# Writing the first two segments of the feed-forward loop into the tail of the attention part

## The chip, the cores and the metric

The kernel runs on one core of a Trainium2 chip, in one launch. The metric is the device time of that core in microseconds. Three runs of the kernel before gave a median of 1109.43 us (1109.27 to 1109.46).

## What is computed

Three stages follow each other on a batch of 4 sequences of 576 tokens, 512 channels wide. The first is attention with random features, for 8 heads of 64 channels and 128 features. The second adds the real part of a Fourier transform over tokens and channels, normalises, and runs a two-layer feed-forward net. The third mixes tokens through a matrix of rank 32 and runs a second net.

```
phi(x) = exp(h - max h) / sqrt(128),   h = x omega^T - |x|^2 / 2
x  = phi(q) (phi(k)^T v) / (phi(q) sum phi(k) + 1e-6)
u  = x + real(fft(fft(x, axis=1), axis=2))
un = (u - mean u) / sqrt(var u + 1e-6)
x  = u + relu(un @ w_ch1) @ w_ch2
u  = x + (x^T U V)^T
out = u + relu(u @ w2_ch1) @ w2_ch2
```

The weights are 512 x 2048 and 2048 x 512 and come as 64-bit floats.

## The kernel before

**Precision.** A product in full precision is made of three: each operand is split into a rounded `hi` and a remainder `lo`, and TensorE adds hi hi, hi lo and lo hi. A split is a copy on ACT and a subtraction on VectorE or GpSimd (`split`, line 119; `wsplit` and `sjob` for weights).

**Weights.** A weight tile (128 x 512) is loaded as 64-bit words (`w_load`), converted with integer steps (`conv_a` and `conv_b`, or in the loop `conv_abs`, `w_conv_exp`, `conv_c` and `conv_d`), kept in one of NSTG staging buffers `w`, and split into the buffers of a ring slot. The ring has RING = 5 slots, weight number f, counted through both layers, goes to slot f mod 5. Slots 0 to 2 lie in the pool `mp`, opened when the attention part's pool `pla` closes; slots 3 and 4 lie in `wbp`, opened when all of the attention part is closed. A conversion needs one buffer named `m` and one named `s` of the pool `cv`, which has two of each. CONV lists the stages of the attention part in which the first eight conversions are written.

**Attention part.** The loop over `n` from line 890 on has 36 stages of 128 tokens, 18 for each pair of batches: nine for keys and values, nine for queries. The transform of the pair is written between the stages, as PLAN says: `fold` adds and subtracts rows of x (F and L), `s_stage` is the transform over tokens (S), `d_stage` over channels (D; r0, r2 and r1 are its three parts, called r stages here), whose results GpSimd adds into `uT`. Ten more rounds (n = 36 to 45, written s = 0 to 9) are the tail: they hold the transform of the last two batches, the split of block 0 (`ln_apply`), and the first steps of the loop. In all of this a planner puts the instructions of each engine in an order of its own, by priority (the order of writing) and by what it takes to be ready; a tile has a name and a fixed number of buffers, and waits for one.

**Feed-forward loop.** The tokens are cut into five blocks of 512, 384, 512, 384 and 512 columns (`BLKS`). The hidden width is cut into 16 parts of 128. A unit is one block and one part; four parts make a group, and a segment is one block with the four parts of a group, so units 0 to 3 are block 0, units 4 to 7 block 1, and so on. `l1(i)` is the first product of a unit, 4 groups of 3 matmuls (lines 760 to 762), and evicts it as `hh` (ACT) and `hl` (VectorE). `l2(i)` is the second, 4 groups of 3 (lines 781 to 783) into four accumulators; after the fourth part VectorE multiplies by 1/deviation (`rs`, line 792), in the first layer, and GpSimd adds to `uT` (line 793). `step(i)` writes l1(i+1) and then l2(i). After each group of three matmuls `tick` is called once: it lets the first job of `jobs` go on to its next `yield`, and in every second call the first of `wjobs`.

**Jobs.** `prep_ln(blk)` makes the statistics of a block: column sums (`s1`), split, a matmul with ones for the mean (lines 596 and 597), then the centred copies `c`, x as `hi` and `lo`, the squares summed on GpSimd (line 616), split, a matmul for the variance (lines 632 and 633), square root and reciprocal. A step may begin block b only when x of that block has been written; if not, it calls `tick` until it has. `wjob` converts a weight of the next group, `sjob` splits it.

**Order.** `step(0)` and `step(1)` (TAIL = 2) are written in rounds s = 2 and 3 of the tail. The rest is a section in which TensorE, ACT, VectorE and GpSimd keep the written order, and in front of it slot 3 is split, as its pool opens there.

Of the kernel before, what the change touches and what calls it, by code (L numbers as in the profile page):

```python
# [26 lines left out]
NBX = 512  # L27
# [13 lines left out]
TAIL = 2  # L41
RING = 5
NSTG = 8
CONV = [1, 4, 5, 8, 20, 26, 31, 33]
# [49 lines left out]
def tile_favor_fnet_moe(ctx: ExitStack, tc: tile.TileContext, qT, kT, v1, om, w1a, w2a, uu, vv, w1b, w2b, cs, cd, out):  # L94
# [97 lines left out]
    def wsplit(fi, k, e=nc.gpsimd):  # L192
        if fi >= 2 * NF or (fi, k) in WS:
            return
        slot = fi % RING
        pool = wpools[0 if slot < 3 else 1]
        hi = pool.tile([128, 512], F32R, tag=f"wh{slot}_{k}", name=f"wh{fi}_{k}")
        lo = pool.tile([128, 512], F32R, tag=f"wl{slot}_{k}", name=f"wl{fi}_{k}")
        split(hi, lo, W.pop(2 * fi + k), e)
        WS[(fi, k)] = hi, lo  # L200
# [211 lines left out]
    def d_stage(b, nm):  # L412
# [10 lines left out]
        qs = plf.tile([128, NEO], F32, tag="qs", name=f"qs{b}{nm}")  # L423
        nc.scalar.activation(qs, pq[0], AF.Copy)
        mm = plf.tile([128, NEO], F32, tag="mm", name=f"mm{b}{nm}")
        pm = plf.tile([128, NEO], F32, tag="pmt", name=f"pm{b}{nm}")
# [14 lines left out]
    omh = ac.tile([128, 256], F32R, tag="omh", name="omh")  # L441
    oml = ac.tile([128, 256], F32R, tag="oml", name="oml")
# [134 lines left out]
    def prep_ln(blk):  # L577
# [16 lines left out]
        yield  # L594
        pmn = misc(f"pmn{blk}")[:, 0:nb]
# [3 lines left out]
        mean = lnt("mean", f"mean{blk}")[:, 0:nb]  # L599
        nc.scalar.activation(mean, pmn, AF.Copy)  # L600
        yield
        hi, lo = x_tiles("x", blk)
# [26 lines left out]
        yield  # L629
        yield  # L630
# [4 lines left out]
        RST[blk] = rs = xps[1].tile([128, nb], F32, tag=f"rs{blk}", name=f"rs{blk}")  # L635
# [108 lines left out]
    prep_at = {(0, 0, 0): [lambda b=b: prep_ln(b + 1) for b in range(1, NBLK - 1)], (0, 1, 0): [mix_consts]}  # L744
# [25 lines left out]
    def l2(*idx):  # L770
# [7 lines left out]
        for r in range(4):  # L778
# [5 lines left out]
            if f % GRP == GRP - 1:  # L784
                cuts = [(0, NB)] if i < NU - 1 or r < 3 else [(0, NB // 2), (NB // 2, NB)]
                for q0, q1 in cuts:
                    u = uT[:, r, c0 + q0 : c0 + q1]
                    if l == 0:
                        while blk not in RS:
                            tick()  # L790
                        t = wpools[1].tile([128, NBX], F32, tag="t", name=f"t{i}_{r}", bufs=2)[:, 0:NB]
# [9 lines left out]
    def wjob(j):  # L801
# [6 lines left out]
        conv_d(*b, nc.gpsimd)  # L808
        yield

    def sjob(fi, k):
        slot = fi % RING
        pool = wpools[0 if slot < 3 else 1]
# [9 lines left out]
    CAT0 = [10, 11, 12, 13, 14, 15, 16, 17]  # L823
    wq_at = {}
    for g in range(2 * NG - 1):
        for q in range(2 * GRP):
            wq_at.setdefault(PER * g + (CAT0[q] if g == 0 else 2 * q), []).append(lambda j=2 * GRP * (g + 1) + q: wjob(j))
# [12 lines left out]
    def tick():  # L840
        turn[0] += 1
        advance(jobs)
        if turn[0] % 2:
            advance(wjobs)

    def step(i):
        l, blk, f = units[i]
        if i == TAIL or (f % GRP == 0 and i > TAIL):
            jobs.extend(g() for g in prep_at.get((l, f // GRP, blk), []))
        if i + 1 < NU:  # L850
# [7 lines left out]
        if i < NU - 2:  # L858
# [31 lines left out]
    for n in range(NS + 10):  # L890
# [50 lines left out]
        else:  # L941
# [14 lines left out]
            if s == 1:  # L956
# [6 lines left out]
                jobs.append(prep_ln(1))  # L963
# [5 lines left out]
            elif 1 <= s < 8:  # L969
# [4 lines left out]
    wsplit(3, 0)  # L974
    wsplit(3, 1)
# [94 lines left out]
```

## Time and profile before

| | us |
|---|---|
| median of three runs | 1109.43 |
| the profiled execution | 1108.71 |
| its span, first to last instruction | 1106.9 |
| TensorE busy (matmuls) | 1054.6 |
| VectorE busy | 589.8 |
| GpSimd busy | 422.1 |
| ACT busy | 403.7 |

The span is that of the profiled execution; 1.8 us of its time lie around it. Line numbers (L760) are those of the kernel before. PE is TensorE, DVE VectorE, POOL GpSimd, SP SyncE. The profile models the end of a matmul, so successive ones overlap in its rows; the distance between their starts is what one costs. PEclk is the granted clock of TensorE as a share of 2.4 GHz.

### The profile page before, as it was taken

How to read it: one execution, taken by the hardware profiler on the slowest of the kernel's cores; microseconds unless marked ns; L12 is line 12 of the kernel's file. 1: busy time of each engine (PE TensorE's matmuls, PEld its weight loads, DVE VectorE, ACT ScalarE, POOL GpSimd, SP SyncE). 2: the span in 40 equal slices, each digit the busy share in tenths (PEclk: the TensorE clock that was granted, in tenths of full speed). 3: DMA queues.
4: the chain of work that ended last, by engine and by line, in shares of the span. 5: the costliest groups of instructions: out<-in, count | busy, mean ns of one | idle time of the engine just before them, and what ended most of it. 6: DMA issues, size and time to landing. Idle time of an engine off the chain costs nothing.

```text
span 1106.9 us, 14702 instructions
## 1 busy us (share of the span) xinstructions
PE 1054.6 (95%) x5656; PEld 926.1 (84%) x5656; DVE 589.8 (53%) x1025; ACT 403.7 (36%) x900; POOL 422.1 (38%) x392
## 2 busy tenths in 40 slices
PE   8999999867699899999999999999999999999998
PEld 7989998756678798889989787788888989888996
DVE  5899878765677465345434465573243423332222
ACT  7887686433343232222222334332222222121110
POOL 3467745654426535534373245431411131131000
PEclk9999998969899999999999999999999999999999
DMA  7632410000003022101101110011111101100111
GB/s 245 209 109 78 134 39 1 1 0 1 1 1 115 24 82 69 39 20 57 57 20 58 38 39 20 20 41 55 39 37 57 41 19 58 47 11 1 67 38 66
DMA packets 47573, 56.86 MB, mean 51 GB/s; under 512 B 3024, under 2 KB 39248, under 8 KB 47376
## 3 DMA queue, kind: packets, MB, share of 16 engines
q1 hardware_dynamic: 47216, 53.23, 15.5%
q0 software_dynamic: 288, 2.70, 0.7%
q8 instruction: 44, 0.72, 0.3%
q14 instruction: 25, 0.20, 0.1%
HBM read 51.20 MB, written 4.72 MB: 51 GB/s over the span
## 4 chain that ended last, share of the span: by engine, by line
PE 80%; DVE 10%; POOL 4%; ACT 2%; issue 1%; DMA 1%; SPq 0%; DVEq 0%; ACTq 0%; POOLq 0%
PE ph L762 11%; PE ph L760 11%; PE ph L761 11%; PE acc L781 11%; PE acc L783 10%; PE acc L782 10%; PE kvp L285 3%; PE pn L322 2%; POOL uT L793 2%; PE pj L258 1%; PE pj L259 1%; PE pj L260 1%; DVE rs L638 1%; PE pt L306 1%; DMA raw<-in_w1a_dram 1%
## 5 line engine op out<-in xcount | busy, mean ns | idle before, releaser
L767 DVE SCALAR_TENSOR_TENSOR hl<-ph,hh 128x512 fp32r<-128x512 f32 (+1 forms) x160 | 101.8, 636 | 377.7 <-ACT hh L766 377.6
L766 ACT ACTIVATE hh<-ph 128x512 fp32r<-128x512 f32 (+1 forms) x160 | 88.6, 554 | 510.3 <-PE ph L762 510.1
L781 PE MATMUL acc<-hh,wh 128*128 128x512 f32 (+1 forms) x640 | 238.8, 373 | 2.5 <-DVE t L792 2.2
L783 PE MATMUL acc<-hl,wh 128*128 128x512 f32 (+1 forms) x640 | 237.2, 371 | 0.0
L782 PE MATMUL acc<-hh,wl 128*128 128x512 f32 (+1 forms) x640 | 236.8, 370 | 0.0
L158 POOL TENSOR_TENSOR w<-mc,sc 128x512 uint32<-128x512 uint32 x56 | 74.1, 1323 | 262.5 <-DVE mc L155 262.5
L793 POOL TENSOR_TENSOR uT<-uT,t 128x512 f32<-128x512 f32 (+1 forms) x80 | 101.7, 1302 | 132.7 <-DVE t L792 132.7
L781 PEld LDWEIGHTS acc<-hh,wh 128*128 128x128 f32 x640 | 120.6, 188 | 21.5 <-DVE t L792 3.9
L783 PEld LDWEIGHTS acc<-hl,wh 128*128 128x128 f32 x640 | 120.2, 188 | 17.1 <-DVE hl L767 0.7
L782 PEld LDWEIGHTS acc<-hh,wl 128*128 128x128 f32 x640 | 120.4, 188 | 15.5
L762 PE MATMUL ph<-xh,wl 128*128 128x512 f32 (+1 forms) x320 | 121.1, 378 | 7.9 <-POOL wl L121 4.3
L761 PE MATMUL ph<-xl,wh 128*128 128x512 f32 (+1 forms) x320 | 120.3, 376 | 1.9 <-DVE xl L121 1.9
L760 PE MATMUL ph<-xh,wh 128*128 128x512 f32 (+1 forms) x320 | 121.2, 379 | 0.7 <-ACT wh L120 0.7
L760 PE MATMUL ph<-yh,wh 128*128 128x512 f32 (+1 forms) x320 | 118.7, 371 | 0.0
L762 PE MATMUL ph<-yh,wl 128*128 128x512 f32 (+1 forms) x320 | 118.6, 371 | 0.0
L761 PE MATMUL ph<-yl,wh 128*128 128x512 f32 (+1 forms) x320 | 118.4, 370 | 0.0
L819 POOL TENSOR_TENSOR wl<-w,wh 128x512 fp32r<-128x512 f32 x56 | 72.4, 1309 | 47.3 <-ACT wh L817 40.0
L274 ACT ACTIVATE phi<-pj,mx 128x128 f32<-128x128 f32 x288 | 82.0, 384 | 9.2 <-DVE mx L263 8.4
L762 PEld LDWEIGHTS ph<-xh,wl 128*128 128x128 f32 x320 | 61.2, 191 | 17.5 <-POOL wl L121 4.7
L761 PEld LDWEIGHTS ph<-xl,wh 128*128 128x128 f32 x320 | 61.3, 191 | 10.3 <-DVE xl L121 2.4
L760 PEld LDWEIGHTS ph<-xh,wh 128*128 128x128 f32 x320 | 61.2, 191 | 9.6 <-ACT wh L120 1.1
L762 PEld LDWEIGHTS ph<-yh,wl 128*128 128x128 f32 x320 | 60.1, 188 | 8.2
(647 smaller groups left out, 1781.1 us busy)
## 6 DMA issues: line engine op xcount, KB each, us to landing
raw<-in_w1a_dram SPq DMA_DIRECT2D x16, 512.0 KB, 3.6
raw<-in_w2a_dram SPq DMA_DIRECT2D x16, 512.0 KB, 3.5
raw<-in_w1b_dram SPq DMA_DIRECT2D x16, 512.0 KB, 3.6
raw<-in_w2b_dram SPq DMA_DIRECT2D x16, 512.0 KB, 3.5
vt<-in_v_dram SPq DMA_DIRECT2D x18, 260.0 KB, 4.0
raw<-in_kT_dram SPq DMA_DIRECT2D x18, 256.0 KB, 2.9
raw<-in_qT_dram SPq DMA_DIRECT2D x18, 256.0 KB, 3.1
out_dram<-uT SPq DMA_DIRECT2D x11, 256.0 KB, 2.1
```

Source lines behind the costliest of these rows:

```text
L158: aeng.tensor_tensor(out=dst.bitcast(U32), in0=mu, in1=s, op=ALU.add)
L274: nc.scalar.activation(phi_[n][:, h, :], pss[g][:, hh, :], AF.Exp, bias=mx[:, h : h + 1])
L760: nc.tensor.matmul(ph, wh[:, c], xh[:, r, :], start=(r == 0), stop=False)
L761: nc.tensor.matmul(ph, wh[:, c], xl[:, r, :], start=False, stop=False)
L762: nc.tensor.matmul(ph, wl[:, c], xh[:, r, :], start=False, stop=(r == 3))
L766: nc.scalar.activation(hh, ph, AF.Relu)
L767: nc.vector.scalar_tensor_tensor(out=hl, in0=ph, scalar=0.0, in1=hh.bitcast(F32), op0=ALU.max, op1=ALU.subtract)
L781: nc.tensor.matmul(a[r], wh[:, c], hh, start=(q == 0), stop=False)
L782: nc.tensor.matmul(a[r], wl[:, c], hh, start=False, stop=False)
L783: nc.tensor.matmul(a[r], wh[:, c], hl, start=False, stop=(q == GRP - 1))
L793: nc.gpsimd.tensor_tensor(out=u, in0=u, in1=t, op=ALU.add)
L819: nc.gpsimd.tensor_tensor(out=lo, in0=src, in1=hi.bitcast(F32), op=ALU.subtract)
```

## The change

Units 0 to 7, two segments, are written into the tail: TAIL becomes 7, so steps 0 to 6 stand in rounds s = 2 to 8, and step 7, the first in the section with a kept order, issues l2(7) ahead of l1(8). Ring slot 3 moves to the pool `mp`, and `rs` of block 1 to the pool that opens with it. There are six staging buffers for weights instead of eight, the small tables `omh` and `oml` lie in the pool that closes early, and the r stages' temporaries `qs` and `pm` lie in the conversions' buffers `s` and `m`. The last two of the first eight conversions move from stages 31 and 33 into round s = 1 of the tail, with the split of slot 3 behind them.

`prep_ln` is cut into `prep_lna` (to the mean) and `prep_lnb` (the rest). Both of block 1 run in the tail; of block 2 the first part runs in the tail and the second is queued in step 7; blocks 3 and 4 are queued when block 2 begins. The pauses ahead of the two matmuls with ones grow from two turns to three and five. The products of units below TAIL use a buffer named `ct`.

In the loop `wjobs` go on in every call of `tick` while more than two are queued. The last two of the eight conversions of a group are queued four units later, behind the first splits. The last addition of the conversions for the second group moves from GpSimd to VectorE.

```diff
@@ -38,10 +38,10 @@
-TAIL = 2
+TAIL = 7
-NSTG = 8
-CONV = [1, 4, 5, 8, 20, 26, 31, 33]
+NSTG = 6
+CONV = [1, 4, 5, 8, 20, 26]
@@ -193,7 +193,7 @@
-        pool = wpools[0 if slot < 3 else 1]
+        pool = wpools[0 if slot < 4 else 1]
@@ -420,10 +420,10 @@
-        qs = plf.tile([128, NEO], F32, tag="qs", name=f"qs{b}{nm}")
+        qs = cv.tile([128, 512], F32, tag="s", name=f"qs{b}{nm}")[:, 0:NEO]
-        pm = plf.tile([128, NEO], F32, tag="pmt", name=f"pm{b}{nm}")
+        pm = cv.tile([128, 512], F32, tag="m", name=f"pm{b}{nm}")[:, 0:NEO]
@@ -438,8 +438,8 @@
-    omh = ac.tile([128, 256], F32R, tag="omh", name="omh")
-    oml = ac.tile([128, 256], F32R, tag="oml", name="oml")
+    omh = pla.tile([128, 256], F32R, tag="omh", name="omh", bufs=1)
+    oml = pla.tile([128, 256], F32R, tag="oml", name="oml", bufs=1)
@@ -574,7 +574,7 @@
-    def prep_ln(blk):
+    def prep_lna(blk):
@@ -592,13 +592,20 @@
+        yield
-        mean = lnt("mean", f"mean{blk}")[:, 0:nb]
+        LN[blk] = mean = lnt("mean", f"mean{blk}")[:, 0:nb]
+
+    def prep_lnb(blk):
+        c0, nb = BLKS[blk]
+        u = uT[:, :, c0 : c0 + nb]
+        add = dict(op=ALU.add)
+        mean = LN.pop(blk)
@@ -626,13 +633,13 @@
-        yield
-        yield
+        for _ in range(5):
+            yield
-        RST[blk] = rs = xps[1].tile([128, nb], F32, tag=f"rs{blk}", name=f"rs{blk}")
+        RST[blk] = rs = xps[0 if blk < 2 else 1].tile([128, nb], F32, tag=f"rs{blk}", name=f"rs{blk}")
@@ -741,7 +748,7 @@
-    prep_at = {(0, 0, 0): [lambda b=b: prep_ln(b + 1) for b in range(1, NBLK - 1)], (0, 1, 0): [mix_consts]}
+    prep_at = {(0, 0, 2): [lambda b=b, p=p: p(b) for b in (3, 4) for p in (prep_lna, prep_lnb)], (0, 1, 0): [mix_consts]}
@@ -788,7 +795,7 @@
-                        t = wpools[1].tile([128, NBX], F32, tag="t", name=f"t{i}_{r}", bufs=2)[:, 0:NB]
+                        t = lnt("ct", f"t{i}_{r}")[:, 0:NB] if i < TAIL else wpools[1].tile([128, NBX], F32, tag="t", name=f"t{i}_{r}", bufs=2)[:, 0:NB]
@@ -805,12 +812,12 @@
-        conv_d(*b, nc.gpsimd)
+        conv_d(*b, nc.vector if j < 4 * GRP else nc.gpsimd)
-        pool = wpools[0 if slot < 3 else 1]
+        pool = wpools[0 if slot < 4 else 1]
@@ -820,11 +827,10 @@
-    CAT0 = [10, 11, 12, 13, 14, 15, 16, 17]
-            wq_at.setdefault(PER * g + (CAT0[q] if g == 0 else 2 * q), []).append(lambda j=2 * GRP * (g + 1) + q: wjob(j))
+            wq_at.setdefault(PER * g + (2 * q if g and q < 6 else 10 + q), []).append(lambda j=2 * GRP * (g + 1) + q: wjob(j))
@@ -840,13 +846,16 @@
-        if turn[0] % 2:
+        if turn[0] % 2 or len(wjobs) > 2:
-        if i == TAIL or (f % GRP == 0 and i > TAIL):
+        if f % GRP == 0 and i > TAIL:
+        if i == TAIL:
+            jobs.append(prep_lnb(2))
+            l2(i)
@@ -855,7 +864,7 @@
-        if i < NU - 2:
+        if i < NU - 2 and i != TAIL:
@@ -960,19 +969,23 @@
-                jobs.append(prep_ln(1))
+                for j in (6, 7):
+                    conv_b(*w_conv_a(j), nc.gpsimd)
+                wsplit(3, 0)
+                wsplit(3, 1)
+                jobs.extend([prep_lna(1), prep_lnb(1)])
-            elif 1 <= s < 8:
+            if s == 6:
+                jobs.append(prep_lna(2))
+            if s >= 1:
-    wsplit(3, 0)
-    wsplit(3, 1)

```

## Rows read from the trace of the kernel before

**Rows 1.** Slices of the page: busy share in tenths, 40 equal parts

```profile
PE   8999999867699899999999999999999999999998
```

**Rows 2.** Waits of TensorE, 170 to 400 us: line, releaser: total us, times, longest

```profile
PE pvr L632 <- ACT hv L626: 7.0, 2, 6.2
PE ps_0o L397 <- ACT zh3o L115: 5.8, 1, 5.8
PE ph L762 <- POOL wl L121: 4.3, 1, 4.3
PE ph L762 <- POOL wl L819: 3.2, 1, 3.2
...
PE pvr L633 <- DVE lv L628: 1.9, 2, 1.6
PE pmn L596 <- ACT hm L590: 1.7, 3, 0.8
```

**Rows 3.** Windows, TensorE: stretch, length, busy (x matmuls), PEclk, DMA, GB/s

```profile
190.00:202.00 12.00, 8.83 (x54) 1.00 0.01 2
...
224.00:230.00 6.00, 0.27 (x1) 0.69 0.00 0
230.00:237.00 7.00, 2.85 (x9) 0.50 0.00 0
237.00:243.30 6.30, 5.80 (x24) 0.50 0.00 0
257.00:261.00 4.00, 3.60 (x10) 0.58 0.02 4
283.00:288.00 5.00, 5.00 (x16) 0.53 0.00 0
379.00:384.00 5.00, 4.85 (x14) 0.66 0.09 32
```

**Rows 4.** Timeline: start, length, engine, line, operation; unit 1 and an eviction

```profile
210.47 0.40 PE L760 MATMUL ph<-xh,wh 128*128 128x512 f32 x1
...
213.24 0.39 PE L781 MATMUL acc<-hh,wh 128*128 128x512 f32 x1
...
226.17 0.68 DVE L767 SCALAR_TENSOR_TENSOR hl<-ph,hh 128x512 fp32r<-128x512 f32 x1
```

**Rows 5.** Timeline, then groups by line (busy us, mean ns): what moves

```profile
256.07 2.50 POOL L121 TENSOR_TENSOR wl<-w,wh 128x512 fp32r<-128x512 f32 x2
...
259.48 2.55 DVE L638 RECIPROCAL rs<-rs 128x384 f32<-128x384 f32 x1 [6.72 <-ACT rs L636]
...
L138 DVE CUSTOM_DVE_ANT_0 w<-mc,sc 128x1024 uint16<-128x1024 uint16 x7 | 7.1, 1018 | 0.0
```

**Rows 6.** Timeline of VectorE and GpSimd: the second statistics of blocks 2 and 3

```profile
266.99 1.29 DVE L609 TENSOR_TENSOR c<-uT,mean 128x512 f32<-128x512 f32 x2 [1.23 <-ACT mean L600]
...
270.35 0.68 DVE L620 TENSOR_TENSOR xl<-c,xh 128x512 fp32r<-128x512 f32 x1
...
270.51 6.73 POOL L793 TENSOR_TENSOR uT<-uT,t 128x512 f32<-128x512 f32 x4 [11.94 <-DVE t L792]
...
276.04 3.43 DVE L620 TENSOR_TENSOR xl<-c,xh 128x512 fp32r<-128x512 f32 x2
...
292.34 1.03 DVE L609 TENSOR_TENSOR c<-uT,mean 128x384 f32<-128x384 f32 x2 [1.06 <-ACT mean L600]
...
297.69 1.84 DVE L620 TENSOR_TENSOR xl<-c,xh 128x384 fp32r<-128x384 f32 x2
```

**Rows 7.** Timeline: the fifth conversion, and the first adds of block 1

```profile
56.46 0.70 ACT L129 ACTIVATE mc<-raw 128x512 f32<-128x512 f32 x1
...
106.20 1.59 DVE L138 CUSTOM_DVE_ANT_0 w<-mc,sc 128x1024 uint16<-128x1024 uint16 x1
...
151.19 0.56 DVE L584 TENSOR_TENSOR s<-uT 128x384 f32<-128x384 f32 x1 [0.70 <-PE pvc L522]
...
192.30 0.53 DVE L583 TENSOR_TENSOR s<-uT 128x384 f32<-128x384 f32 x1
```

## The prediction, made before the changed kernel was run

> **What bounds the kernel now.** The slices of the page come first: TensorE is busy 0.9 or more of nearly every slice, except at both ends and from the sixth to the eleventh [rows 1]. So the reader is to see that the time is TensorE's work plus what it loses in one stretch, about 190 to 385 us, where the attention part hands over to the feed-forward loop. TensorE's waits there come next [rows 2], longest first, and then the windows [rows 3], which show a second loss: after a long wait the granted clock is at 0.50, the lower of its levels (1.2 GHz), and the matmuls that follow take twice as long. The change can give back these two things only; the matmuls stay the same in number and shape.
>
> **What can be given back.**
> (a) The transform of the last batch waits for its folds (lines 397 and 399; the longest single wait is 5.8 us [rows 2]). From 224 to 243.3 us TensorE is idle 5.73 + 4.15 + 0.50 = 10.4 us [rows 3]. It has nothing else to do: only units 0 to 2 of the loop are in the attention part (TAIL = 2), and they are used up.
> (b) Unit 3 waits 4.3 us for the lo part of its weights [rows 2]: slot 3 lies in memory that opens when the attention part is closed, so that split stands behind the last additions on GpSimd.
> (c) The variance sum of block 2 (line 632) waits 6.2 us, the longest of two that make 7.0 [rows 2].
> (d) Unit 22 waits 3.2 us for a weight split (line 819) [rows 2]. I counted the turns of the job lists in the code: with one turn in every second group of three matmuls, weight 6's split comes only in the loop that unit 22 itself waits in. With a turn in every group while more than two jobs are queued, the same count puts it at units 19 and 20, and the wait goes.
> (e) The clock, as busy time times what the granted clock lacks of 1, in the five windows at a low clock from 230 us on [rows 3]: 2.85 x 0.50 + 5.80 x 0.50 + 3.60 x 0.42 + 5.00 x 0.47 + 4.85 x 0.34 = 9.7 us. Each part goes with the wait ahead of it.
> Sum: 10.4 + 4.3 + 6.2 + 3.2 + 9.7 = 33.8 us.
>
> **What moves, and what it costs.** *The tail.* Units 3 to 7 are now written into it. Half a unit is 12 matmuls, 210.47 to 213.24 us, so 2.77 us at 512 columns [rows 4], and three quarters of it, 2.08, at 384. Moved are three halves of block 0 and seven of block 1: 3 x 2.77 + 7 x 2.08 = 22.9 us, more than the 14.7 of (a) and (b). But not all of it fits there. In the tail the first product has one PSUM buffer, so a unit starts only when VectorE has evicted the one before, and it does so late: the eviction of unit 2 ran at 226.17 [rows 4], when TensorE had run dry. So unit 3 starts near 227 and unit 4 some 6 us later, about half of the gap stays, and the other units run behind the folds, between the transform's steps. The same stretch also gets two weight conversions (four steps on ACT, six on VectorE, two on GpSimd, their loads on SyncE), two splits (ACT, and 2.50 us on GpSimd), and the square root and reciprocal of block 1 (ACT; 2.55 on VectorE) [rows 5]. ACT and SyncE have room, and the load that is queued behind is needed only at unit 10. On VectorE the six steps (at most 1.02 each, as the dearest step of a conversion [rows 5]) and the reciprocal are up to 8.7 us among the folds, which end the wait (a); where VectorE is idle now they cost nothing, and I take 3 to 5 us. The conversions have a new wait, for a buffer that the r stages of batch 2 use (lines 423 and 426); ACT's copies of these stages stand behind it, and TensorE's transform behind those. For what stays lost in the tail, idle and clock, I take 9 us. Bounds: the window 190 to 202 us, which is mixed in this way already, is idle 3.2 us [rows 3]; with nothing filled it is (a) with its clock, 10.4 + 4.3 = 14.7.
>
> *The new wait.* The loop reaches block 2 with the second part of the statistics only just begun: step 7 queues it, issues l2(7), and then drives it with no unit in between until x of block 2 is written. VectorE has four centred copies, four lo parts and four products of unit 7, GpSimd four additions and three sums, each in order. This chain took from 266.99 to 276.04 + 3.43 = 12.5 us in block 2, beside GpSimd's additions (four in 6.73 us), and from 292.34 to 297.69 + 1.84 = 7.2 us in block 3, without them [rows 6]. I take 10.5: the additions are there, but 384 columns wide. The chain starts some 0.6 us into l2(7), and l1(8) can follow x row by row, so l2(7) (2.1) and l1(8) (2.8) are hidden, with one group (0.7) at the end: 0.6 + 10.5 + 0.7 - 2.1 - 2.8 = 6.9 us. As that is as long as (c), whose clock cost 5.00 x 0.47, I add 2.1: 9.0 us. Bounds: 3.6 (7.2 us of chain, no clock) to 11.2 (12.5 and 2.3).
> Here a page speaks against the change. The rows show a lo part at 0.68 us, and two in 3.43 us beside GpSimd [rows 6]. The Trainium skill, "SBUF — State Buffer", section "Who interferes with whom", has it that a VectorE instruction with two inputs in SBUF and a GpSimd instruction that reads SBUF contend, and one blocks for the whole of the other; the rows agree. By that rule throughout, the chain would be the long one of block 2 and the result 2 us worse.
>
> *Later statistics.* The pauses ahead of lines 596 and 632 grow, but the chains behind them (sums, split, square root, reciprocal) are as long as before, and blocks 3 and 4 come about as much nearer to their use. Now these waits are 7.0 - 6.2 + 1.9 + 1.7 = 4.4 us [rows 2]; counting groups between neighbouring sums I get about as much again. Net 0, bounds -4 (all covered) to +4. The last add of eight conversions moves from GpSimd to VectorE (8 x 1.02 [rows 5]), beside TensorE's work; if it delays block 4, that is in the +4. The later place of the last two conversions in each group costs nothing: by the count no later unit waits for a weight, and if one did it would cost about (d).
>
> Sum: 33.8 - 9.0 - 9.0 - 0 = 15.8 us. From the profiled execution's 1108.7 this gives 1092.9; the median of the runs is 0.7 above it, so 1093.6, said as 1093.
>
> **The rivals.**
> (1) VectorE binds the tail. The folds come later, nothing more is filled, and the chain of block 2 is at its long end: 33.8 - 14.7 - 11.2 = 7.9 us of gain, 1101. For it: the late eviction [rows 4]. Against: the planner puts units where TensorE is free.
> (2) Everything is covered: 33.8 - 3.2 - 3.6 + 4 = 31.0, 1078. For it: 22.9 us of units for a gap of 14.7.
> (3) Slower. The r stages now share two pairs of buffers with the weight conversions. A conversion starts as early as its data allows and then waits: the fifth began on ACT at 56.46 and wrote its weight at 106.20 [rows 7], with a pair held for 50 us. The last two now can't end before a weight buffer (six instead of eight) is freed by the loop's first splits, after 190 us. If they take both pairs before the last r stage of batch 1, this stage waits some 50 us with two of the three PSUM buffers; transposes and copies then alternate on the third. At half speed that is 25 us lost, and block 1's statistics come too late to fill the tail, 14.7 - 9 = 6 more: 31 against a gain of 16, 1124. It decides once that stage waits over 25 us. Against: tiles of one name seem to take buffers in the order in which they are written. The two adds of block 1's statistics are neighbours in the code, yet one ran at 151.19 and the other, whose buffer the folds written ahead of it also use, at 192.30 [rows 7]. Then the conversions stand behind the r stages and block none of those written ahead.
> (4) The gain is lost in a new order of the attention part: within 0.2%, 1109.
>
> **How the numbers follow.** 0.2% (2.2 us) is about what a measurement of this kernel can tell from no change. Forecast (12 to 25 us of gain) 0.56; rival 1 0.17; rival 2 0.10; rival 3 0.11; rival 4 0.06. Faster 0.83, same 0.06, slower 0.11. The range reaches from rival 2 to a little past rival 1, 1078 to 1104, and leaves out rivals 3 and 4, 0.17.
>
> **What would show it.** Units 3 to 7 stand among the matmuls of lines 397 to 420; no wait of line 762 for a split at line 121 in unit 3; a wait of 4 to 9 us ahead of unit 8 for block 2's lo part, right behind l2(7); no wait for line 819; unit 8 starts some 15 us earlier than now. I am wrong in the tail if the folds end past 245 us, in the new wait if it is over 11 us, and in the whole if the r stages of batch 1 come later than now.

## The result and the profile after

The changed kernel takes 1092.5 us (median of four runs, 1089.7 to 1094.6) where the kernel before took 1109.45 beside it: a ratio of 0.985 (95% interval 0.982 to 0.987). Forecast were 1093 us and a range of 1078 to 1104. The sum was right. One term was out by 9.5 us, and gains beyond the forecast elsewhere made up for it. The profiled execution took 1093.14 us with a span of 1091.4.

| us | before | after |
|---|---|---|
| span of the profiled execution | 1106.9 | 1091.4 |
| TensorE busy | 1054.6 | 1051.1 |
| VectorE busy | 589.8 | 596.8 |
| GpSimd busy | 422.1 | 412.2 |

The slices of the page of the changed kernel, the line that answers [rows 1]; line numbers below are those of the changed kernel (L767 to L769 are the first product, L788 to L790 the second):

```profile
PE   8999999889788999999999999999999999999998
```

The gap from the eighth to the eleventh slice (8, 6, 7 and 6 tenths before) is mostly closed (8, 8, 9 and 7), but the twelfth and thirteenth slices are now at 8. Waits of TensorE from 170 to 400 us, the view of [rows 2] (line, releaser: total us, times, longest):

```profile
PE pmn L597 <- ACT hm L590: 4.9, 2, 3.7
PE ph L768 <- DVE xl L627: 4.5, 3, 1.7
PE ph L767 <- DVE hl L774: 2.9, 1, 2.9
...
PE acc L790 <- DVE hl L774: 1.6, 1, 1.6
...
PE pvr L640 <- DVE lv L635: 1.2, 1, 1.2
PE pvr L639 <- ACT hv L633: 1.1, 1, 1.1
PE acc L788 <- DVE t L799: 1.0, 2, 0.6
```

The four longest waits of before (7.0 and 5.8 us, and two for weights) are gone or down to 1.1 us. New are the mean sum of block 4 (L597, 3.7 us) and block 2's lo parts (L627, three waits). The windows of TensorE (stretch, length, busy, granted clock, DMA share, GB/s), to be laid beside [rows 3]:

```profile
224.00:230.00 6.00, 3.07 (x14) 0.97 0.00 0
230.00:237.00 7.00, 6.71 (x26) 0.78 0.00 1
237.00:243.30 6.30, 4.96 (x20) 0.73 0.00 0
...
270.00:280.00 10.00, 5.57 (x18) 0.70 0.00 0
280.00:290.00 10.00, 9.50 (x33) 0.78 0.00 0
```

From 224 to 243.3 us TensorE now has 4.6 us of idle time in place of 10.4. What the change brought in is the loss from 270 to 290 us, the wait for block 2.

For the balance the starts of units serve best: the work between two of them is the same in both kernels. The starts of the first products of units 0, 7, 9, 20 and 24 on TensorE's timeline, before:

```profile
193.91 0.50 PE L760 MATMUL ph<-xh,wh 128*128 128x512 f32 x1
...
289.34 0.34 PE L760 MATMUL ph<-xh,wh 128*128 128x384 f32 x1
...
300.20 0.39 PE L760 MATMUL ph<-xh,wh 128*128 128x512 f32 x1
...
364.26 0.39 PE L760 MATMUL ph<-xh,wh 128*128 128x512 f32 x1
...
391.44 0.34 PE L760 MATMUL ph<-xh,wh 128*128 128x384 f32 x1
```

and after:

```profile
194.16 0.50 PE L767 MATMUL ph<-xh,wh 128*128 128x512 f32 x1
...
265.36 0.33 PE L767 MATMUL ph<-xh,wh 128*128 128x384 f32 x1
...
283.16 0.63 PE L767 MATMUL ph<-xh,wh 128*128 128x512 f32 x1
...
356.69 0.39 PE L767 MATMUL ph<-xh,wh 128*128 128x512 f32 x1
...
378.61 0.34 PE L767 MATMUL ph<-xh,wh 128*128 128x384 f32 x1
```

| stretch | before | after | gain | forecast, from its terms |
|---|---|---|---|---|
| unit 0 to 7 | 95.43 | 71.20 | +24.2 | +20.0: (a) 10.4, (b) 4.3, (c) 6.2, clock 8.1, tail -9.0 |
| unit 7 to 9 | 10.86 | 17.80 | -6.9 | -9.0: the new wait |
| unit 9 to 20 | 64.06 | 73.53 | -9.5 | 0: later statistics |
| unit 20 to 24 | 27.18 | 21.92 | +5.3 | +4.9: (d) 3.2, clock 1.7 |
| unit 24 to the end | 715.5 | 712.8 | +2.7 | 0 |

With 0.25 us lost ahead of unit 0 this is 15.5 us of span, against 15.8 forecast. The third line is the failure, and the question for the runs: what do units 9 to 20 wait for? The gain behind unit 24 was not forecast; 1.1 us of it came with the denser turns alone (e1_pace, below), and the rest is not explained.

### The profile page after: what moved, and what is told of

Its sections match the earlier page's. It is cut to its first block, busy times and chain, and to the rows that moved or that the text cites. A ratio compares the mean times of both kernels' runs of the same rounds, so it can differ in the third digit from the quotient of the medians.

```text
span 1091.4 us, 14695 instructions
## 1 busy us (share of the span) xinstructions
PE 1051.1 (96%) x5656; PEld 925.5 (85%) x5656; DVE 596.8 (55%) x1031; ACT 404.3 (37%) x900; POOL 412.2 (38%) x386
## 3 DMA queue, kind: packets, MB, share of 16 engines
q1 hardware_dynamic: 47216, 53.23, 15.5%
## 4 chain that ended last, share of the span: by engine, by line
PE 84%; DVE 9%; POOL 3%; ACT 2%; issue 2%; DMA 1%; SPq 0%; DVEq 0%; ACTq 0%; POOLq 0%
PE ph L768 11%; PE ph L769 11%; PE ph L767 11%; PE acc L790 11%; PE acc L788 11%; PE acc L789 11%; PE kvp L285 3%; PE pn L322 2%; PE pj L258 1%; PE pj L259 1%; PE pj L260 1%; PE pt L306 1%; DVE rs L645 1%; POOL uT L438 1%; PE mt L703 1%
## 5 line engine op out<-in xcount | busy, mean ns | idle before, releaser
L788 PE MATMUL acc<-hh,wh 128*128 128x512 f32 (+1 forms) x640 | 238.0, 372 | 1.0 <-DVE t L799 1.0
L790 PE MATMUL acc<-hl,wh 128*128 128x512 f32 (+1 forms) x640 | 236.6, 370 | 1.6 <-DVE hl L774 1.6
L158 POOL TENSOR_TENSOR w<-mc,sc 128x512 uint32<-128x512 uint32 x48 | 62.6, 1304 | 217.8 <-DVE mc L155 212.4
L788 PEld LDWEIGHTS acc<-hh,wh 128*128 128x128 f32 x640 | 120.5, 188 | 18.6 <-DVE t L799 1.9
L790 PEld LDWEIGHTS acc<-hl,wh 128*128 128x128 f32 x640 | 120.2, 188 | 18.4 <-DVE hl L774 2.5
L768 PE MATMUL ph<-xl,wh 128*128 128x512 f32 (+1 forms) x320 | 122.5, 383 | 6.5 <-DVE xl L627 4.5
L767 PE MATMUL ph<-xh,wh 128*128 128x512 f32 (+1 forms) x320 | 122.5, 383 | 3.3 <-DVE hl L774 2.9
L769 PE MATMUL ph<-xh,wl 128*128 128x512 f32 (+1 forms) x320 | 121.5, 380 | 0.5 <-DVE wl L121 0.5
L767 PE MATMUL ph<-yh,wh 128*128 128x512 f32 (+1 forms) x320 | 118.7, 371 | 0.0
L769 PE MATMUL ph<-yh,wl 128*128 128x512 f32 (+1 forms) x320 | 118.6, 371 | 0.0
L826 POOL TENSOR_TENSOR wl<-w,wh 128x512 fp32r<-128x512 f32 x56 | 74.9, 1354 | 70.5 <-ACT wh L824 59.7
L767 PEld LDWEIGHTS ph<-xh,wh 128*128 128x128 f32 x320 | 62.1, 194 | 13.0 <-DVE hl L774 3.3
L769 PEld LDWEIGHTS ph<-xh,wl 128*128 128x128 f32 x320 | 62.2, 194 | 8.9 <-DVE wl L121 0.8
L769 PEld LDWEIGHTS ph<-yh,wl 128*128 128x128 f32 x320 | 60.1, 188 | 8.2
```

Of the source, the lines that this page charges most:

```text
L158: aeng.tensor_tensor(out=dst.bitcast(U32), in0=mu, in1=s, op=ALU.add)
L767: nc.tensor.matmul(ph, wh[:, c], xh[:, r, :], start=(r == 0), stop=False)
L768: nc.tensor.matmul(ph, wh[:, c], xl[:, r, :], start=False, stop=False)
L769: nc.tensor.matmul(ph, wl[:, c], xh[:, r, :], start=False, stop=(r == 3))
L788: nc.tensor.matmul(a[r], wh[:, c], hh, start=(q == 0), stop=False)
L790: nc.tensor.matmul(a[r], wh[:, c], hl, start=False, stop=(q == GRP - 1))
```

## Experiments

Each kernel was timed in turns with the kernel before. Runs of one kernel spread by 1 to 10 us (more on this at the end), so small effects are read from the starts of units and from TensorE's idle time in the profile. The changed kernel was run a second time (e11_again) for the size of that uncertainty.

| run | median us | ratio to before, 95% | 0 to 7 | 7 to 9 | 9 to 20 | 20 to 24 |
|---|---|---|---|---|---|---|
| the changed kernel | 1092.5 | 0.982 to 0.987 | 71.20 | 17.80 | 73.53 | 21.92 |
| e11_again, the same | 1091.3 | 0.980 to 0.984 | 72.54 | 17.81 | 74.79 | 21.92 |
| e1_pace | 1105.2 | 0.991 to 0.996 | 96.25 | 10.53 | 64.06 | 22.00 |
| e2_addpool | 1090.6 | 0.978 to 0.984 | 71.17 | 17.80 | 72.16 | 21.92 |
| e3_norecip | 1087.7 | 0.975 to 0.980 | 72.53 | 17.80 | 72.01 | 21.93 |
| e4_tail5 | 1090.4 | 0.979 to 0.983 | 72.76 | 11.62 | 76.99 | 21.92 |
| e5_noconv | 1089.1 | 0.978 to 0.985 | 72.53 | 17.81 | 68.94 | 21.92 |
| e6_tail5q | 1090.5 | 0.979 to 0.984 | 71.18 | 13.20 | 75.74 | 21.92 |
| e7_late | 1085.2 | 0.975 to 0.979 | 71.20 | 11.63 | 69.33 | 24.38 |
| e8_noadd7 | 1090.7 | 0.978 to 0.987 | 72.49 | 14.95 | 74.70 | 21.92 |
| e9_recip4 | 1079.9 | 0.969 to 0.974 | 73.99 | 11.54 | 67.80 | 21.92 |
| e10_sumpool | 1079.6 | 0.969 to 0.973 | 74.00 | 11.55 | 66.54 | 21.92 |
| e12_noconv67 | 1094.2 | 0.982 to 0.986 | 72.58 | 17.80 | 74.68 | 21.92 |

The last four columns are worked out from the starts of units in each profiled execution. The two profiled executions of the changed kernel differ by 1.3 us in the first and third of them: smaller differences say nothing there.

**One part alone: the turns of the weight jobs (e1_pace).** The kernel before with one line of the change:

```diff
-        if turn[0] % 2:
+        if turn[0] % 2 or len(wjobs) > 2:
```

> The kernel before with one part of the change alone: the weight jobs get a turn in every group while more than two are queued. Theory (term d of the prediction): weight 6 is split before unit 22 needs it, the wait of 3.2 us for line 819 goes with the slow clock behind it (5.00 x 0.34 = 1.7 us), nothing else moves: 1109.45 - 4.9 = 1104.5. Rival: the denser turns put steps of conversions ahead of the statistics of blocks 3 and 4 in VectorE's queue; what unit 22 gives back is lost there (waits for hm, hv, lv and hl between 290 and 350 us grow by 4 us or more): 1108 to 1110.

Measured: 7.2 us less than before by the medians (interval 4.4 to 9.9), 5.2 of them between units 20 and 24; units 9 to 20 take 64.06 us, to the last digit as in the kernel before. The window that held the wait of 3.2 us is full:

```profile
360.00:400.00 40.00, 40.00 (x191) 1.00 0.20 56
```

Term (d) is confirmed, and the rival falls: denser turns for the weights do not disturb the statistics in the order that the kernel before has. The loss in units 9 to 20 needs the new order.

**VectorE's share of the loss (e2_addpool, e3_norecip, e5_noconv).** The timeline of the changed kernel at the end of block 2, where the mean sum of block 4 waits: VectorE's rows from 308.76 to 313.51 us, with the square root on ACT ahead of them (start, length; in brackets the idle time before it and its releaser):

```profile
307.69 0.58 ACT L643 ACTIVATE rs<-pvr,epst 128x384 f32<-128x384 f32 x1 [1.91 <-PE pvr L640]
...
308.76 0.69 DVE L799 TENSOR_TENSOR t<-acc,rs 128x512 f32<-128x512 f32 x1 [0.59 <-POOL uT L800]
309.37 1.16 DVE L158 CUSTOM_DVE_ANT_0 w<-mc,sc 128x1024 uint16<-128x1024 uint16 x1
310.45 0.68 DVE L799 TENSOR_TENSOR t<-acc,rs 128x512 f32<-128x512 f32 x1
311.05 2.54 DVE L645 RECIPROCAL rs<-rs 128x384 f32<-128x384 f32 x1
313.51 0.62 DVE L583 TENSOR_TENSOR s<-uT 128x512 f32<-128x512 f32 x1
...
315.55 0.63 ACT L590 ACTIVATE hm<-s 128x512 fp32r<-128x512 f32 x1 [6.15 <-DVE s L586]
...
316.23 0.80 PE L597 MATMUL pmn<-hm,onesr 128*128 128x512 f32 x1 [3.69 <-ACT hm L590]
```

The reciprocal of block 3, the products of block 2 and a conversion stand ahead of the sums of block 4. The square root of block 3 is done on ACT at 307.69 + 0.58 = 308.27 us, and the reciprocal starts on VectorE 2.8 us later, behind two products and the addition of a conversion; the product at 308.76 has itself waited 0.59 us for GpSimd. In the kernel before, VectorE was idle when this square root ended and began at once:

```profile
304.20 2.55 DVE L638 RECIPROCAL rs<-rs 128x384 f32<-128x384 f32 x1 [0.68 <-ACT rs L636]
```

The wait ahead of the mean sum of block 4 was at most 0.8 us there [rows 2] and is 3.7 here, 2.9 more. From 310 to 350 us VectorE is busy 94% of the time:

```profile
310.00:350.00 40.00, 37.52 (x48) 0.91 0.22 71
```

Three runs took work out of this queue.

```diff
-        conv_d(*b, nc.vector if j < 4 * GRP else nc.gpsimd)
+        conv_d(*b, nc.gpsimd)
```

> The changed kernel, with the last addition of the conversions 8 to 15 back on GpSimd, nothing else undone. Theory (VectorE's queue sets the mean of block 4): the addition of 1.16 us that stood between the square root and the reciprocal of block 3 leaves the queue, the wait of 3.7 us ahead of the mean sum of block 4 shrinks by 1 to 1.5 us and others between 330 and 350 us by about as much: 1090 to 1091. Rival: VectorE waits there for GpSimd's products anyway; the additions lengthen GpSimd's queue and the additions of the residual with it: 1092.5 to 1095.

```diff
-        nc.vector.reciprocal(out=rs, in_=rs)
+        if blk < 3:
+            nc.vector.reciprocal(out=rs, in_=rs)
```

> The changed kernel without the reciprocals of blocks 3 and 4 (2 of 2.54 us on VectorE; these blocks are then scaled by the standard deviation). Theory: the reciprocal of block 3 stands ahead of the sums of block 4 in VectorE's queue, so the wait ahead of the mean sum of block 4 goes from 4.5 us to 2 us, the slow clock behind it (2.3 us) mostly goes too, and 1 us more comes from block 4's: 1087 to 1089. Rival: the late start of block 4's statistics is set by the pauses and the order of the job list; then the wait shrinks by less than 1 us and the time stays within 1091.5 to 1092.5.

```diff
-        b = w_conv_exp(*a)
-        yield
-        conv_c(*b)
+        if j < 4 * GRP:
+            b = a[0], a[1], a[2].bitcast(U32), a[3]
+            yield
+        else:
+            b = w_conv_exp(*a)
+            yield
+            conv_c(*b)
```

> The changed kernel without three of the four VectorE steps of the conversions 8 to 15 (lines 149, 151 and 155: 0.43 + 0.43 + 0.68 = 1.54 us for each; these weights then have wrong values). Theory (from about 290 to 350 us the loop is bound by VectorE, which is busy 9.0 to 9.8 tenths from 310 to 350 us): 8 x 1.54 = 12.3 us leave its queue, the waits of TensorE in 300 to 350 us (9.4 us idle and 2.3 us of clock) fall to half or less: 1086 to 1087. Rival (the length of the statistics' chains in turns of the job list sets the waits): they change by less than 2 us: 1091 to 1093.

TensorE between the starts of units 9 and 20, in the kernel before, the changed kernel and e5_noconv:

```profile
300.20:364.26 64.06, 58.96 (x272) 1.00 0.16 50
```

```profile
283.16:356.69 73.53, 62.76 (x275) 0.95 0.16 51
```

```profile
280.27:349.21 68.94, 62.46 (x276) 0.94 0.19 56
```

| units 9 to 20 | length, us | TensorE idle | granted clock | VectorE busy |
|---|---|---|---|---|
| the kernel before | 64.06 | 5.1 | 1.00 | 46.5 |
| e1_pace | 64.06 | 5.1 | 1.00 | 52.5 |
| the changed kernel | 73.53 | 10.8 | 0.95 | 60.8 |
| e2_addpool | 72.16 | 8.8 | 0.92 | 58.4 |
| e3_norecip | 72.01 | 6.9 | 0.90 | 56.8 |
| e5_noconv | 68.94 | 6.5 | 0.94 | 48.1 |

So of the 9.5 us lost 5.7 are idle time, and the rest is the lower clock that comes with the waits (0.50 from 315.0 to 321.8 us). Work taken from VectorE gives back most of the idle time, but by length only about half of the loss: 4.6 to 5.9 us in e5_noconv, against the two executions of the changed kernel (2 to 3 by the medians, in which it can't be told from them). The amount of VectorE's work alone does not make the rest. In e5_noconv VectorE does about as much as in the kernel before, and the stretch is still 4.9 us longer; in e1_pace it is busy 82% of the stretch, as in the changed kernel (83%), and nothing is lost.

The theories' details do not hold either. The waits ahead of the mean sums of blocks 3 and 4, 5.8 us in the changed kernel, stay at 5.9, 5.2 and 5.4 us in the three runs; what vanished without the reciprocals were other waits: 1.6 us for hl, 1.0 for t and 0.8 of the 1.1 for hv. The wait ahead of the mean sum of block 4 went only from 4.5 to 4.0 us in e3_norecip, not to 2; in this the rival was right, though the median, 1087.7, lies in the theory's range. The rows show why. Without the reciprocal the sums of block 4 come while GpSimd still adds the products of block 2, and take 1.18 and 1.75 us in place of 0.62 and 0.67, so 1.6 of the 2.5 us go there (how GpSimd holds VectorE up is shown at e8_noadd7):

```profile
313.50 1.18 DVE L583 TENSOR_TENSOR s<-uT 128x512 f32<-128x512 f32 x1
314.60 1.75 DVE L584 TENSOR_TENSOR s<-uT 128x512 f32<-128x512 f32 x1
```

In e2_addpool the longest wait stays as well (3.8 us): the addition is gone from VectorE, but GpSimd has it now, the last two products wait 0.59 and 0.56 us for GpSimd, and the first sum takes 1.16 us. By these rows the wait is set by the chain from block 3's variance to block 4's mean, which runs over VectorE and GpSimd in turn; how much of the 9.5 us is their order and how much VectorE's load, no single run separates.

**Two units kept back (e4_tail5, e6_tail5q).**

```diff
-TAIL = 7
+TAIL = 5
```

> The changed kernel with five instead of seven steps of the loop in the tail (units 6 and 7 are left for the time behind it). Theory: between 243 and 270 us TensorE is full in any case, so two units fewer there cost at most 3 us of waits between the transform's steps, while they cover the second statistics of block 2: the wait of 4.9 us ahead of unit 8 and its clock (3.8 us) go, 8.7 - 3 = 5.7: 1086 to 1088. Rival: the transform's last steps then wait for VectorE's splits and the tail loses what the chain gives back: 1091 to 1094, with waits in lines 397 to 424 grown by 5 us or more.

The new wait went as the theory has it: 17.80 to 11.62 us between units 7 and 9. The tail gave back nothing that can be seen (72.76, against 71.20 and 72.54). But units 9 to 20 took 2 to 3.5 us more. Waits of TensorE from 270 to 360 us in this run:

```profile
PE pmn L597 <- ACT hm L590: 6.4, 2, 3.9
PE pmn L598 <- DVE lm L592: 2.8, 2, 2.7
```

The mean sums of blocks 3 and 4 now wait for 9.2 us together (5.8 in the changed kernel). Neither side was right: the place named by the rival, the transform, lost nothing, but what block 2 gave back was partly lost in blocks 3 and 4. The next run has the same five steps, and the other statistics are queued at unit 5:

```diff
-    prep_at = {(0, 0, 2): [lambda b=b, p=p: p(b) for b in (3, 4) for p in (prep_lna, prep_lnb)], (0, 1, 0): [mix_consts]}
+    prep_at = {(0, 1, 0): [mix_consts]}
...
             jobs.append(prep_lnb(2))
+            jobs.extend(p(b) for b in (3, 4) for p in (prep_lna, prep_lnb))
```

> The changed kernel with five steps in the tail, and the statistics of blocks 3 and 4 queued right behind those of block 2 (at unit 5, not at unit 8). Theory (the start of the chains sets the waits): block 2 stays covered as with five steps alone, the chains of blocks 3 and 4 start up to two units earlier, and of the 13 us lost between 290 and 350 us in the changed kernel at least 6 go: 1083 to 1086. Rival (VectorE's load is the bound): the same work stands in the same stretch, the waits only move: 1089 to 1091.

Measured 1090.5, as the rival has it. The reason is simpler than either theory: the list is worked off in order, and block 2's second part fills it until unit 8. The mean sum of block 3 stood 90.65 us behind the start of unit 0, and 91.87 in e4_tail5, in both behind the same 75 groups of three matmuls of the loop; to queue the jobs earlier changed nothing.

**Relieving VectorE (e7_late, e9_recip4, e10_sumpool).** With five steps in the tail and the statistics queued as in e6_tail5q, the conversions 8 to 15 were moved by two units, the splits of these weights by one, and the conversions' last addition back to GpSimd:

```diff
-        conv_d(*b, nc.vector if j < 4 * GRP else nc.gpsimd)
+        conv_d(*b, nc.gpsimd)
...
-            wq_at.setdefault(PER * g + (2 * q if g and q < 6 else 10 + q), []).append(lambda j=2 * GRP * (g + 1) + q: wjob(j))
+            wq_at.setdefault(PER * g + (2 * q if g and q < 6 else 10 + q + (0 if g else 2)), []).append(lambda j=2 * GRP * (g + 1) + q: wjob(j))
...
-                wq_at.setdefault(PER * g + 15 + q, []).append(lambda fi=GRP * (g + 1) + q, k=k: sjob(fi, k))
+                wq_at.setdefault(PER * g + (15 if g else 16) + q, []).append(lambda fi=GRP * (g + 1) + q, k=k: sjob(fi, k))
```

> As the run with five steps and all statistics queued at unit 5, and besides the conversions 8 to 15 start two units later and their last addition is on GpSimd. Theory (VectorE's load): 2 to 3 us less than that run, as conversions no longer stand among the statistics of block 4: 1081 to 1084. Rival: the weights of units 20 to 23 come late (waits for lines 119 and 826 before unit 20), 2 us more than that run: 1086 to 1089.

1085.2 us, 5 less than e6_tail5q and between the two ranges, with units 9 to 20 at 69.33 in place of 75.74; the rival is right too, on a smaller scale: one weight came 2.1 us late (L826), and units 20 to 24 took 24.38. The next run moves the conversions by one unit only, leaves the splits where the changed kernel has them, and cuts the reciprocal:

```diff
-        nc.vector.reciprocal(out=rs, in_=rs)
+        for c in range(0, nb, nb // 4):
+            nc.vector.reciprocal(out=rs[:, c : c + nb // 4], in_=rs[:, c : c + nb // 4])
+            yield
...
-            wq_at.setdefault(PER * g + (2 * q if g and q < 6 else 10 + q), []).append(lambda j=2 * GRP * (g + 1) + q: wjob(j))
+            wq_at.setdefault(PER * g + (2 * q if g and q < 6 else 10 + q + (0 if g else 1)), []).append(lambda j=2 * GRP * (g + 1) + q: wjob(j))
```

> As the run with the conversions two units later (1085.2 us), but one unit later, and every reciprocal of the statistics in four parts with a turn between them. Theory (a long instruction in VectorE's queue holds up short ones that TensorE waits for): the wait of 2.1 us for weights of unit 22 goes, and of the 7.3 us ahead of the mean sums of blocks 3 and 4 about 2: 1081 to 1083. Rival (only the amount of VectorE's work counts): four parts cost as much as one or more, the waits stay: 1084 to 1087.

1079.9 us: more than the theory gave, and the weight is in time. But its reason is not borne out. The reciprocal of block 2 and the mean sum of block 3, in e7_late:

```profile
277.60 3.34 DVE L645 RECIPROCAL rs<-rs 128x512 f32<-128x512 f32 x1
...
283.08 0.45 PE L597 MATMUL pmn<-hm,onesr 128*128 128x384 f32 x1 [2.50 <-ACT hm L590]
```

and in e9_recip4:

```profile
280.76 3.38 DVE L646 RECIPROCAL rs<-rs 128x128 f32<-128x128 f32 x4
...
286.87 0.45 PE L597 MATMUL pmn<-hm,onesr 128*128 128x384 f32 x1 [0.34 <-ACT hm L590]
```

The four parts ran back to back, and nothing passed between them. From the start of the reciprocal to the mean sum it takes 6.1 us, 5.5 in e7_late; the wait fell from 2.50 to 0.34 us all the same. The four turns more put the mean sum four groups of matmuls later in TensorE's order: 79 groups of the loop stand ahead of it in the trace, 75 in e7_late. I take this for the cause; it is not shown by itself, as e9_recip4 moves the conversions too and no run has four empty turns and a whole reciprocal.

The last of these runs adds to e9_recip4:

```diff
-        nc.vector.tensor_tensor(out=s2, in0=u[:, 2, :], in1=u[:, 3, :], **add)
+        (nc.gpsimd if blk > 2 else nc.vector).tensor_tensor(out=s2, in0=u[:, 2, :], in1=u[:, 3, :], **add)
+        if blk > 2:
+            yield
```

> As the run with the reciprocals in four parts, and one of the three sums that open the statistics of blocks 3 and 4 is on GpSimd, ahead of the other two (0.49 and 0.68 us leave VectorE, 1.5 us come to GpSimd). Theory (VectorE's load): the waits ahead of the two mean sums shrink by 0.5 to 1 us each: 1 to 2 us less than that run. Rival: GpSimd still has the additions of the block's residual in its queue, the sum comes later than on VectorE: 1 to 3 us more than that run.

1079.6 us, the same as without it; by the medians neither theory can be told from no effect. The waits ahead of the two mean sums fell from 4.2 to 2.5 us, but the edit adds a turn as well, so this is not shown to be VectorE's load. TensorE's idle time in units 9 to 20 is 5.2 us here, that of the kernel before, with VectorE busy 53.4 us. This kernel and e9_recip4 beat both kernels: 0.971 of before (intervals 0.969 to 0.973 and 0.969 to 0.974), and about 1% below the changed kernel run beside them (1091.3).

**The chain of block 2 (e8_noadd7).** VectorE and GpSimd in the new wait, in the changed kernel:

```profile
270.72 0.68 DVE L616 TENSOR_TENSOR c<-uT,mean 128x512 f32<-128x512 f32 x1
...
270.88 5.62 POOL L800 TENSOR_TENSOR uT<-uT,t 128x384 f32<-128x384 f32 x4 [0.92 <-DVE t L799]
...
272.74 0.55 DVE L799 TENSOR_TENSOR t<-acc,rs 128x384 f32<-128x384 f32 x1
273.21 1.02 DVE L627 TENSOR_TENSOR xl<-c,xh 128x512 fp32r<-128x512 f32 x1
...
278.65 3.43 DVE L627 TENSOR_TENSOR xl<-c,xh 128x512 fp32r<-128x512 f32 x2
```

The second of the four additions, by itself:

```profile
272.22 1.45 POOL L800 TENSOR_TENSOR uT<-uT,t 128x384 f32<-128x384 f32 x1
```

The run leaves the four additions out:

```diff
-                        nc.gpsimd.tensor_tensor(out=u, in0=u, in1=t, op=ALU.add)
+                        if i != 7:
+                            nc.gpsimd.tensor_tensor(out=u, in0=u, in1=t, op=ALU.add)
```

> The changed kernel without GpSimd's four additions behind the products of unit 7 (5.62 us from 270.88 us on; the first part of block 1's residual is left out). Theory (VectorE's steps of block 2's chain are held up while GpSimd adds): the chain from the first centred copy to the last lo part goes from 11.4 us to about 8, the loss ahead of units 8 and 9 (4.9 us idle, 3.8 us of clock) from 8.7 to about 4: 1087 to 1089. Rival (VectorE's own twelve instructions make the chain): the chain stays above 10.5 us, the time within 1091 to 1093.

The same stretch in e8_noadd7:

```profile
275.69 0.68 DVE L616 TENSOR_TENSOR c<-uT,mean 128x512 f32<-128x512 f32 x1
...
277.82 0.68 DVE L627 TENSOR_TENSOR xl<-c,xh 128x512 fp32r<-128x512 f32 x1
...
281.84 2.37 DVE L627 TENSOR_TENSOR xl<-c,xh 128x512 fp32r<-128x512 f32 x2
```

From the first centred copy to the last lo part it takes 281.84 + 2.37 - 275.69 = 8.5 us, and 278.65 + 3.43 - 270.72 = 11.4 with the additions. The theory holds for the chain. Units 7 to 9 gained 2.9 us (17.80 to 14.95), as much as the chain, where the theory had 4.7; the clock over this stretch was still at 0.88 (0.74 with the additions). The median, 1090.7, lies between the two ranges.

The rows show how GpSimd holds VectorE up. The first lo part takes 0.68 us alone and 1.02 beside GpSimd. It starts at 273.21 us, under the addition that ends at 272.22 + 1.45 = 273.67, and it ends at 274.23, 0.56 us after that. From 271.78 to 282.09 us seven of VectorE's eight copies and lo parts start under an instruction of GpSimd, and each ends 0.55 us after that instruction. VectorE's products, which read one input from PSUM, take 0.55 us beside the same additions. The Trainium skill, "SBUF — State Buffer", section "Who interferes with whom", says that a VectorE instruction with two inputs in SBUF contends with a GpSimd instruction that reads SBUF, for ports that are an exclusive lock. The two traces agree: a copy or lo part is held until the running GpSimd instruction ends, and the first lo part lost only 0.34 us because that addition had 0.46 us left. In e8_noadd7 the three sums of GpSimd are still there, and still hold up what starts under them.

**The conversions in the tail (e12_noconv67).**

```diff
-                    conv_b(*w_conv_a(j), nc.gpsimd)
+                    w_load(j + 1)
+                    W[j] = wap.tile([128, 512], F32, tag="w", name=f"w{j}", bufs=NSTG)
+                    a = conv_abs(W[j], raws.pop(j), 0, 512, 128, f"c{j}")
+                    conv_d(a[0], a[1], a[2].bitcast(U32), a[3], nc.gpsimd)
```

> The changed kernel without the three VectorE steps of the two conversions in the tail (lines 131, 133 and 137; these two weights then have wrong values). Theory (the prediction's 3 to 5 us that the tail's added VectorE work costs): the folds end some 2 to 3 us earlier, TensorE's loss between 210 and 270 us (6.3 us idle, 3.3 us of clock) falls by 2 to 4 us: 1089 to 1091. Rival (they run at 208 to 212 us, where VectorE was idle before the change): the loss falls by less than 1 us: 1092 to 1094.

The rival is right: unit 0 to 7 takes 72.58 us, 72.54 in e11_again beside it; TensorE's waits from 210 us on are the same to 0.1 us. In the changed kernel these steps run from 208 to 212 us; in the kernel before VectorE was idle for 1.1 and 2.5 us between 210 and 214.

**The changed kernel again (e11_again).**

> The changed kernel once more, beside the others of this call. Theory (its runs differ by the granted clock of the attention part, which the change doesn't touch): the median is 1090 to 1094 again with a spread of some 5 us; TensorE's idle time by stretch repeats to 1 us, and only the clock's loss between 30 and 190 us differs by several us. Rival: the idle time itself differs from run to run, by 2 us or more between 210 and 360 us.

The median, 1091.3, and the idle time repeat about as the theory has it: from 210 to 270 us TensorE is idle 7.4 us here and 6.3 in the first execution, from 300 to 360 us 9.1 and 9.4. From 30 to 190 us the granted clock differs: 0.96 in the first execution and 0.98 here, which over 156 us is 3 us. But the idle time differs there too (3.4 and 4.8 us), and unit 0 starts only 0.7 us earlier; so the clock is not the only thing that differs in the attention part, as the theory had it.

## Why the prediction was right, point by point

**What bounds the kernel, (a) to (e).** Right. The waits of (a) to (d) are gone or down to what was said, and (d) was measured alone at 5.2 us against 4.9 with its clock. Three slips cost nothing: the slices below 0.9 are the eighth to the eleventh and the fourteenth, not the sixth to the eleventh [rows 1]; the products of (e) add up to 9.8 us, not 9.7; and the 1.02 us taken as the most for a conversion's step is a mean, [rows 7] has one of 1.59.

**The tail.** Right in sum: idle 6.3 us from 210 to 270 us and, from the two windows at 0.78 and 0.73, 6.71 x 0.22 + 4.96 x 0.27 = 2.8 us of clock, 9.1 against 9.0. The named mechanism is there, too: TensorE waits 2.9 us for unit 2's eviction. Wrong is the part put down to the conversions' steps: they cost nothing (e12_noconv67). The folds ended at 243.7 us, inside the bound of 245, but 7 us later than before: the reciprocal of block 1, from 240.59 on, stood ahead of the last fold's lo part in VectorE's queue. Unit 0 to 7 gained 4.2 us more than forecast. From the start of unit 0 to that of unit 7 TensorE was idle 26.0 us before, of which (a) to (c) are 20.9: the terms were the longest waits, and the small ones shrank with them, to 8.9 us in all.

**The new wait.** Right in sum: the chain took 11.4 us (10.5 taken, bounds 7.2 and 12.5). Units 7 to 9 hold 2.08 + 2.08 + 2.77 + 2.08 = 9.0 us of matmuls by the prediction's own prices, so 8.8 us are lost, against 9.0; 1.9 of that was lost there before, so the net cost is 6.9. It was made up otherwise than forecast (6.9 us idle and 2.1 of clock): from unit 7 to 9 TensorE is idle 4.9 us, and the clock is 0.74. Unit 8 itself started 23 us earlier (295.29 to 272.12), not some 15, and then waited for its lo parts. The contention that the prediction held against the change was there, and GpSimd's four additions made 2.9 us of the 11.4 (e8_noadd7).

**Later statistics.** This is the term that was mis-sized: 0, with -4 to +4 as bounds, and it cost 9.5 us. The step that failed is the claim that the chains of blocks 3 and 4 stand as long as before, a bit nearer to their use. It counted turns of the job list and took VectorE's time for each turn as given. In the new order block 3's reciprocal starts 2.8 us after its square root, behind the products of block 2, which wait for GpSimd, and an addition of a conversion; the mean sum of block 4 waits 2.9 us longer for it, and the slow clock follows. Less work on VectorE gave back about half of the loss (e5_noconv). In the new order the waits ahead of the two mean sums fell below 5 us only where more groups of matmuls stand between a block's variance and the next mean: 9 groups in the changed kernel (5.8 us), 13 in e9_recip4 (4.2), 14 in e10_sumpool (2.5); the kernel before had 8 groups and waited 1.7. That the order makes the other half is argued, not shown by a run of its own. The sentence "if it delays block 4, that is in the +4" saw the place and gave it too little.

**The rivals.** (1) VectorE does not bind the tail; its queue, with GpSimd's additions, does delay the stretch behind it: much of the right mechanism, in the wrong place. (3) does not occur. The r stages of batch 1 read their sums on VectorE at 124.26, 132.03 and 143.18 us, before at 123.44, 131.27 and 142.46: 0.7 to 0.8 us later, not 50. By its words the last sign of being wrong was met, but in e11_again, the same kernel, they came at 121.90, 129.51 and 140.63, earlier than before: so small a shift lies within what two executions of one kernel differ by. The conversions 6 and 7 started on ACT at 207.24 and 209.26 us, released by GpSimd's last additions of batch 2: behind the r stages, in the written order.

**So** the forecast of 15.8 us was met at 15.5 because 4.2 + 2.1 + 0.4 + 2.7 us of gains beyond the forecast stood against 9.5 + 0.25 of loss. That was luck in the sum; the step on the later statistics has no part in it.

## What to carry to other kernels

When work is moved on the engine that bounds, draw up the load of the engine that feeds it in the new order, window by window: a helper at 55% of the whole span was at 94% in the 40 us that mattered. Then look at what stands ahead of each step that the bounding engine waits for, as the load alone misleads: over units 9 to 20 VectorE was as busy in e1_pace, which lost nothing. A chain of statistics needs room in two queues, the time its steps take on VectorE and, as far as e9_recip4 tells, the number of groups that TensorE has ahead of the matmul that closes it; to queue the job earlier, behind one that is still at work, buys neither (e6_tail5q). Keep as many units back as the longest chain behind the hand-over lasts: five steps in the tail cost nothing there that can be seen and covered block 2, though blocks 3 and 4 then lost 2 to 3.5 us of it.

## What the runs showed of the hardware

Much of the spread of the runs comes from TensorE's clock. TensorE from 210 to 222 us, in the two profiled executions of the same kernel, first the changed kernel and then e11_again:

```profile
210.00:222.00 12.00, 10.21 (x53) 1.00 0.25 89
```

```profile
210.00:222.00 12.00, 10.17 (x47) 0.86 0.25 89
```

The idle time is the same to 0.04 us, yet in one execution the clock stayed at the upper of its two levels, and in the other a part of the stretch ran at the lower one. From the start of unit 0 to that of unit 3 both are idle 7.25 us, at a clock of 0.95 and 0.90, and take 34.14 and 35.68 us. In the ten profiled executions of the changed kernel and its variants with whole reciprocals units 0 to 7 took 71.2 us four times and 72.5 to 72.8 six times, and nothing in between. From 30 to 190 us, which no experiment touches, the mean clock lay between 0.95 (e8_noadd7) and 0.99 (e5_noconv): 156 us of matmuls x 0.04 = 6 us between two executions, for reasons that no row here shows; their units 0 start at 197.84 and 189.93 us. So a change of 2 us in this kernel is seen in the starts of units, not in four runs.

An addition or subtraction of VectorE (512 columns) with two inputs in SBUF that starts under one of GpSimd's additions or sums ends 0.55 us after it: seven in a row in the chain of block 2, which took 11.4 us so and 8.5 without the four additions. The wait is part of the instruction's length in the profile, 1.02 to 1.76 us in place of 0.68.

A reciprocal of 512 columns on VectorE takes 3.34 us in one part and 3.38 in four; its price is by the column, five times that of a centred copy (0.68).
